# Operand splits on ScalarE and VectorE instead of GpSimd, and two experts of the second chunk in three passes

## The chip, the cores and the metric

The kernel runs on one core of a Trainium2 chip. A core has five engines that work side by side, each through its own queue of instructions in order: TensorE (PE, with PEld for the load of its stationary operand), VectorE (DVE), ScalarE (ACT), GpSimd (POOL) and SyncE (SP, which here only starts DMA transfers). [...] The metric is the device time of one launch in microseconds (us). A lower time is better.

## The reference

Two blocks follow each other.

```python
# attention with sketched features, per batch b (4) and head h (4), 1088 tokens, 32 dimensions
phi(x) = outer(S1 x, S2 x)              # 8 * 8 = 64 features
kv = sum_s phi(k_s) v_s^T ;  z = sum_s phi(k_s)
attn = (phi(q) kv) / (phi(q) z + 1e-6)
x = attn as (4352 tokens, 128)          # heads side by side
# four experts over every token, 128 -> 1024 -> 128
p = domain_probs / (sum of domain_probs + 1e-9)
out = sum_e p[:, e] * (relu(x @ w1[e]) @ w2[e])
```

Everything is float32. Nearly all of the arithmetic is the experts' two products.

## The kernel before, in words

**Tiling.** The 4352 tokens are cut into eleven chunks of 128, 448, 512 (six times), 320, 256 and 128 columns (`CHUNKS`), numbered 0 to 10. For each chunk the kernel walks over 4 experts and, within one, over 4 pairs of 128-wide hidden blocks: `NQ` = 16 steps a chunk, 176 in all, numbered through, so chunk 1 is steps 16 to 31 and chunk 2 begins at step 32. A step i does the first product of two hidden blocks (`first`, j = 0 and 1) and, `LA` = 2 steps behind, the second product of step i-2 (`second`). Between and after the two blocks of a step it writes pieces of the attention (`work`, `piece`): the attention of later tokens runs inside the experts' loop, at a rate worked out from what the coming chunks need. The schedule is written by hand: each engine's queue holds its instructions in the order in which the code writes them.

**Exactness.** In this trace a float32 matmul of 448 columns is followed by the next after 0.750 us, and one of 512 columns on operands of the type fp32r after 0.233 us; the code rounds its operands before it uses that type, hence the splits. Chunks 0 and 10 (`plain`) and chunk 1 (`whole`) use plain float32 matmuls: line 898 for the first product, line 984 for the second. In the others the first product is three fp32r passes over split operands: weights and tokens are each cut into a rounded part and its remainders (`wa`, `wb`, `wd`; `xa`, `xb`, `xd`), line 911 multiplies wa by xa, line 912 wb by xb, ACT scales the sum in place (line 913), and line 931 (`third`) adds wd by xd one block later. Of the second products, those with an even block number (`in_three`) have three passes too (lines 994, 995 and 1001), with hidden values split by ACT (line 935, ha) and DVE (lines 936 and 937, hb and hd in the profile); the odd ones are float32 (line 1001, hid by w_sb).

**Banks.** First products land in four PSUM banks (`ps_h`) that are reused in turn, two a step. In `whole` steps an expert's sum lies in one of two banks, o0 or o1, in turn; with three passes each expert uses both. When an expert closes (`gather`), ACT copies o0 or o1 (line 1028 or 1030), DVE adds o1 (line 1031, three passes only), and POOL multiplies by the gate and adds to the total (lines 1035, 1037, 1038).

**Splitting.** `weight_parts(e)` makes wa, wb and wd of an expert in four steps (two halves); `second_weight_parts(e)` makes vab and vd for the even blocks of w2, writing over buffers of w1 and w2 that are no longer read; `token_parts(m)` makes xa, xb and xd of a chunk. In all three, ACT (line 706, `scaled`, and lines 717, 734, 758) writes scaled copies and rounded parts, and POOL (line 710, `minus`) subtracts. The scaled copies lie in the buffers `ob`, `ev` and `ew`; `ob` and `ev` are those that line 1010 and lines 1028 to 1038 use as well. `to_part` says which expert's splits are written after which step: weights of expert e at steps 16+4e to 19+4e, second weights from step 24+4e. Token splits of chunk m+1 are written after step 12 of chunk m (counted from 0), behind attention pieces that are made up for there.

**Attention on DVE and PE.** Keys: transposes (lines 367, 372), projections on PE (line 410), an addition (420), eight products (425), sums on PE (line 226, in `key_sum`). Queries: a transpose (522), a projection on PE (666), shuffles and an addition (669 to 679), four products qp (535), matmuls n and f (line 226, in `attend`), then division and transposition.

Of the kernel before, what the change touches and what calls it, by code (L numbers as in the profile page):

```python
# [8 lines left out]
F32 = mybir.dt.float32  # L9
BF16 = mybir.dt.bfloat16  # L10
F32R = mybir.dt.float32r
I32 = mybir.dt.int32
ALU = mybir.AluOpType
ACTF = mybir.ActivationFunctionType
# [10 lines left out]
def kernel(  # L25
# [24 lines left out]
    nc = tc.nc  # L50

    P = 128
    HP = 64
    B, H, S, D = q.shape
    E, DM, F = w1.shape
# [6 lines left out]
    NQ = E * FB // 2  # L62
# [636 lines left out]
    wb = cpool.tile([P, E, F], F32R, name="wb")  # L699
    wd = cpool.tile([P, E, F], F32R, name="wd")  # L700

    def scaled(tag, w, scale, dtype=F32):

        t = mpool.tile([P, CW], F32, tag=tag, bufs=1, name="tw")[:, :]
        t = t[:, 0 : w.shape[-1]]
        nc.scalar.activation(t.bitcast(dtype), w, ACTF.Copy, scale=scale)
        return t

    def minus(out, in0, in1):
        nc.gpsimd.tensor_tensor(out=out, in0=in0, in1=in1, op=ALU.subtract)  # L710

    def weight_parts(e):

        HF = F // 2
        for c in (slice(0, HF), slice(HF, F)):
            w, a, b, d = (x[:, c] for x in (w1_of[e], wa[:, e], wb[:, e], wd[:, e]))
            nc.scalar.activation(a, w, ACTF.Copy, scale=4096.0 * NEAR)
            minus(b, scaled("ob", w, 4096.0), a.bitcast(F32))
            yield
            minus(d, b.bitcast(F32), scaled("ev", w, NEAR, F32R))  # L720
            yield


# [3 lines left out]
    def second_weight_parts(e):  # L727

        w = w2_of[e, 0]
        vab = cpool.tile([P, 2, KS * NK * DM], F32R, tag=f"w1_{e}", name="vab")  # L730
        a, b = vab[:, 0], vab[:, 1]
        minus(b, scaled("ob", w, 4096.0), scaled("ev", w, 4096.0 * NEAR, F32R))
        yield
        nc.scalar.activation(a, w, ACTF.Copy, scale=NEAR)
        d = cpool.tile([P, KS * NK * DM], F32R, tag=f"w2_{e}0", name="vd")[:, :]
        minus(d, b.bitcast(F32), a.bitcast(F32))
        w2_parts[e] = a, b, d
        yield

# [13 lines left out]
    def token_parts(m):  # L753

        n = CHUNKS[m]
        xa, xb, xd_ = (mpool.tile([P, CW], F32R, tag=f"x{i}", name=f"x{i}") for i in "abd")
        ((x, _, _),) = placed(START[m], n)
        nc.scalar.activation(xa[:, 0:n], x, ACTF.Copy, scale=R12 * NEAR)
        minus(xb[:, 0:n], x, scaled("ew", x, NEAR, F32R))
        minus(xd_[:, 0:n], xa[:, 0:n].bitcast(F32), xb[:, 0:n].bitcast(F32))  # L760
        xparts[m] = xa, xb, xd_

    def start():

# [76 lines left out]
    def plain(m):  # L841
        return m in (0, NC - 1)

    def whole(m):
        return m == 1

    begun_hp, made_hp = {}, {}

# [12 lines left out]
    def first(i, work, between=None):  # L861

        m, kq = steps[i]
        n, (e, f) = CHUNKS[m], divmod(kq, NP)
        if plain(m):
            third()
            hd = hidden()
            hid[i] = [hd[:, n * j : n * j + n] for j in range(2)]
            if i in begun_hp:
                hp = begun_hp.pop(i)  # L870
                half_columns(i, hp, HP)
            elif i in made_hp:
                hp = made_hp.pop(i)
            else:
                hp = psum(ps_h, "h")
                for j in range(2):
                    both(
                        hp[:, n * j : n * j + n],
                        w1_of[e][:, P * (2 * f + j) : P * (2 * f + j + 1)],
                        (x_last if m else x_first)[:, :],  # L880
                        start=True,
                        stop=True,
                    )
            if m and kq % 2:
                nc.vector.tensor_scalar(
                    out=hd[:, 0 : 2 * n], in0=hp[:, 0 : 2 * n], scalar1=0.0, scalar2=None, op0=ALU.max
                )
            else:
                nc.scalar.activation(hd[:, 0 : 2 * n], hp[:, 0 : 2 * n], ACTF.Relu)
            work()  # L890
            work()
            return
        hid[i] = []
        if whole(m):
            ((x, _, _),) = placed(START[m], n)
            for j in range(2):
                hp = psum(ps_h, "h")[:, 0:n]
                nc.tensor.matmul(hp, w1_of[e][:, P * (2 * f + j) : P * (2 * f + j + 1)], x, start=True, stop=True)
                u = hidden()[:, 0:n]
                nc.scalar.activation(u, hp, ACTF.Relu)  # L900
                hid[i].append(u)
                work()
                if between and j == 0:
                    between(0)
            return
        xa, xb, xd_ = (x[:, 0:n] for x in xparts[m])
        for j in range(2):
            k = 2 * f + j
            g = psum(ps_h, "h")[:, 0:n]
            w = slice(P * k, P * (k + 1))  # L910
            nc.tensor.matmul(g, wa[:, e, w], xa, start=True, stop=False)  # L911
            nc.tensor.matmul(g, wb[:, e, w], xb, start=False, stop=True)  # L912
            nc.scalar.activation(g, g, ACTF.Copy, scale=1.0 + R12)  # L913
            third()
            hid[i].append(None)
            begun.append((i, j, k, g, wd[:, e, w], xd_))
            work()
            if between and j == 0:
                between(0)
# [25 lines left out]
    def second(i, j=None):  # L945
# [4 lines left out]
        if plain(m):  # L950
# [24 lines left out]
                    t, to = (B * S - P, [[DM, P], [1, DM]]) if m else (0, [[G * DM, 32], [1, 4 * DM]])  # L975
                    nc.sync.dma_start(bass.AP(out.tensor, out.offset + t * DM, to), total.pop(m)[:, :])
            return
        if whole(m):
            if f == 0 and j == 0:
                acc[m, e] = None, psum(ps_o, f"o{e % 2}")  # L980
            for j in range(2) if j is None else (j,):
                k = 2 * f + j
                o1 = acc[m, e][1][:, 0:n]
                nc.tensor.matmul(o1, second_weight(e, k), hd[j], start=(k == 0), stop=(k == FB - 1))  # L984
            return
# [82 lines left out]
        begun_hp[i] = psum(ps_h, "h")  # L1068
        half_columns(i, begun_hp[i], 0)
    to_part = {}  # L1070
    for e in range(E):
        for at, parts_of in ((NQ + 4 * e, weight_parts(e)), (NQ + 8 + 4 * e, second_weight_parts(e))):
            for x in range(4):
                to_part.setdefault(at + x, []).append(parts_of)
    ending = iter(())

    def close(i):
# [6 lines left out]
    for i in range(len(steps) + LA):  # L1084
        if i < len(steps):
            m, kq = steps[i]
            while have[0] < START[m] + CHUNKS[m]:
                piece()

            gone = START[m] + CHUNKS[m] * kq / NQ  # L1090
            left = lambda c: START[c] - (4 if c > 1 else 0) * CHUNKS[c - 1] / NQ - gone
            rate = CHUNKS[m] / NQ * max(
                [0] + [(needed[c] + (8 if c > 1 else 4) - done[0]) / left(c) for c in range(m + 1, NC) if left(c) > 0]
            )

            def work():

                if not NQ <= i < NQ + 2:
                    credit[0] = min(credit[0] + rate / 2, 2)
                while credit[0] >= 1:  # L1100
                    credit[0] -= 1
                    piece()

            parted = i >= LA and not plain(steps[i - LA][0]) and not plain(m)
            closing = parted and steps[i - LA][1] % NP == NP - 1

            def between(j):

                if closing:
                    second(i - LA)  # L1110
                    close(i - LA)
                else:
                    second(i - LA, j)

            first(i, work, between if parted else None)
            for parts_of in to_part.get(i, ()):
                next(parts_of, None)
            if kq == NQ - 4 and 0 < m < NC - 2:
                while have[0] < START[m + 1] + CHUNKS[m + 1]:
                    piece()  # L1120
                token_parts(m + 1)
            if i == 2:
                gate_quotients()
            elif i == 5:
                store_gates()
                load_gates(1, range(E))
                load_batch(1)
            if m == NC - 2 and kq == NQ // 2:
                while have[0] < B * S:
                    piece()  # L1130
                load_last()
        if i == LA:

            made_hp[3] = psum(ps_h, "h")
            for c in (0, HP):
                half_columns(3, made_hp[3], c)
        if i >= LA:
            parted = i < len(steps) and parted
            mm, kk = steps[i - LA]
            if parted and closing:  # L1140
                continue
            second(i - LA, 1 if parted else None)
            if kk % NP == NP - 1 and not plain(mm):
                close(i - LA)
            else:
                next(ending, None)
# [29 lines left out]
```

## Time and profile before

| | |
|---|---|
| time, median of 3 runs | 485.01 us (484.96 to 485.11) |
| time of the profiled execution | 485.2 us |
| its span, first to last instruction | 483.4 us |
| TensorE matmuls (PE) busy | 471.4 us, 98% |
| weight loads (PEld) busy | 330.8 us, 68% |
| VectorE (DVE) busy | 327.2 us, 68% |
| ScalarE (ACT) busy | 331.2 us, 69% |
| GpSimd (POOL) busy | 141.9 us, 29% |
| granted TensorE clock | 1.00 |

A line of a group or timeline names the engine, the line of the kernel, the operation and the tiles, written before read. `[0.63 <-ACT h L913]` says that the engine stood idle for 0.63 us until ACT's instruction of line 913 was done. Matmuls are pipelined, so their durations overlap; the distance from start to start tells what one costs. Busy shares are averages over the whole span, and stages differ: between 71 and 84 us, in chunk 1, PE was busy for 13.00 of 13.00 us, POOL for 11.09, ACT for 8.73 and DVE for 0.00; between 96 and 109 us, in chunk 2, PE was busy for 11.09 of 13.00 and DVE for 12.57.

### The profile page before, as it was taken

Reading aid. Unit: us, or ns where it says so; the run is one execution under the profiler, and the core shown is the slowest. Engines: PE = TensorE matmul, PEld = TensorE weight load, DVE = VectorE, ACT = ScalarE, POOL = GpSimd, SP = SyncE. Lnnn points to the kernel's source line nnn. Section 1 sums busy time; section 2 is a strip of 40 time slices with the busy share of each in tenths; the row PEclk is TensorE's granted clock in tenths of the full one; section 3 lists DMA queues with packets and bytes.
Section 4 is the critical chain, followed back from the end, with each engine's and each line's share of the span. In section 5 each row is a group of like instructions: output and inputs, shape, how many; then the busy total and the mean of one; then the engine's idle time right before and its main releaser. Section 6 shows DMA issues by size and latency. Waiting matters only on the chain.

```text
span 483.4 us, 8071 instructions
## 1 busy us (share of the span) xinstructions
PE 471.4 (98%) x2845; PEld 330.8 (68%) x2845; DVE 327.2 (68%) x615; ACT 331.2 (69%) x696; POOL 141.9 (29%) x149
## 2 busy tenths in 40 slices
PE   8999999989999999999999999999999999999997
PEld 5965555656666676666666676667666666888987
DVE  6833250696877769687887669597877686765652
ACT  4366676876857777676857777676877686888841
POOL 5134478432222124211322124212331032232120
PEclk9999999999999999999999999999999999999999
DMA  7827204411101212411103210013102100120710
GB/s 225 273 69 159 66 22 87 97 42 23 44 23 49 45 44 65 118 24 41 41 23 65 45 33 24 22 17 45 38 24 58 29 14 15 34 57 22 244 34 18
DMA packets 45472, 29.19 MB, mean 60 GB/s; under 512 B 26264, under 2 KB 40952, under 8 KB 45432
## 3 DMA queue, kind: packets, MB, share of 16 engines
q1 hardware_dynamic: 45416, 28.68, 23.6%
q8 instruction: 22, 0.36, 0.3%
q14 instruction: 18, 0.15, 0.1%
q10 hardware_dynamic: 16, 0.00, 0.0%
HBM read 24.42 MB, written 4.24 MB: 59 GB/s over the span
## 4 chain that ended last, share of the span: by engine, by line
PE 66%; DVE 6%; ACT 5%; issue 2%; ACTq 0%; DVEq 0%
PE o L1001 23%; PE h L931 10%; PE h L912 8%; PE h L911 8%; PE o L994 5%; PE o L995 5%; ACT h L913 3%; PE n L226 2%; PE h L226 2%; PE o L226 1%; DVE qp L535 1%; DVE hd L937 1%; DVE kp L425 1%; PE f L666 1%; DVE hb L936 1%
## 5 line engine op out<-in xcount | busy, mean ns | idle before, releaser
L913 ACT ACTIVATE h<-h 128x512 f32<-128x512 f32 (+2 forms) x256 | 138.0, 539 | 100.6 <-PE h L912 91.6
L936 DVE SCALAR_TENSOR_TENSOR hb<-h,ha 128x512 fp32r<-128x512 f32 (+2 forms) x128 | 80.8, 631 | 92.3 <-ACT ha L935 91.8
L911 PE MATMUL h<-xa,wa 128*128 128x512 f32 (+2 forms) x256 | 140.5, 549 | 0.0
L1001 PE MATMUL o<-hid,w_sb 128*128 128x512 f32 (+2 forms) x256 | 119.2, 547 | 0.0
L937 DVE SCALAR_TENSOR_TENSOR hd<-ha,hb 128x512 fp32r<-128x512 f32 (+2 forms) x128 | 98.8, 772 | 8.4
L931 PE MATMUL h<-xd,wd 128*128 128x512 f32 (+2 forms) x256 | 98.3, 384 | 3.2 <-ACT h L913 1.5
L912 PE MATMUL h<-xb,wb 128*128 128x512 f32 (+2 forms) x256 | 94.2, 368 | 0.0
L1037 POOL TENSOR_TENSOR ev<-ev,gate 128x512 f32<-128x512 f32 (+3 forms) x27 | 31.3, 1159 | 153.8 <-DVE ev L1031 153.1
L943 ACT ACTIVATE hid<-h 128x512 f32<-128x512 f32 (+2 forms) x128 | 70.2, 548 | 0.2 <-PE h L931 0.2
L935 ACT ACTIVATE ha<-h 128x512 fp32r<-128x512 f32 (+2 forms) x128 | 69.9, 546 | 0.0
L911 PEld LDWEIGHTS h<-xa,wa 128*128 128x128 f32 x256 | 48.2, 188 | 30.1 <-issue 18.6
L912 PEld LDWEIGHTS h<-xb,wb 128*128 128x128 f32 x256 | 48.3, 189 | 29.3 <-issue 23.6
L931 PEld LDWEIGHTS h<-xd,wd 128*128 128x128 f32 x256 | 48.0, 188 | 23.7 <-ACT h L913 16.0
L1001 PEld LDWEIGHTS o<-hid,w_sb 128*128 128x128 f32 x256 | 45.9, 188 | 8.1
L1001 PE MATMUL o<-hd,vd 128*128 128x512 f32 (+2 forms) x128 | 48.3, 378 | 2.7 <-DVE ev L1031 2.7
L994 PE MATMUL o<-ha,vab 128*128 128x512 f32 (+2 forms) x128 | 50.6, 395 | 0.0
L995 PE MATMUL o<-hb,vab 128*128 128x512 f32 (+2 forms) x128 | 47.4, 370 | 0.0
L1038 POOL TENSOR_TENSOR total<-total,ev 128x512 f32<-128x512 f32 (+3 forms) x27 | 35.4, 1313 | 2.1
L535 DVE TENSOR_TENSOR qp<-qa,qb 64x512 f32<-64x512 f32 (+5 forms) x44 | 33.1, 753 | 1.0
L1035 POOL TENSOR_TENSOR total<-ev,gate 128x512 f32<-128x512 f32 (+3 forms) x9 | 10.5, 1163 | 70.3 <-issue 34.0
L1001 PEld LDWEIGHTS o<-hd,vd 128*128 128x128 f32 x128 | 24.0, 187 | 9.3 <-DVE ev L1031 4.5
L984 PE MATMUL o<-hid,w_sb 128*128 128x448 f32 x64 | 28.9, 544 | 0.0
(150 smaller groups left out, 545.4 us busy)
## 6 DMA issues: line engine op xcount, KB each, us to landing
gate<-gates SPq DMA_DIRECT2D x16, 256.0 KB
kn<-in_k_dram SPq DMA_DIRECT2D x4, 544.0 KB
vn<-in_v_dram SPq DMA_DIRECT2D x16, 128.0 KB
w_sb<-in_moe_w_dram SPq DMA_DIRECT2D x4, 512.0 KB
w_sb<-in_moe_w_dram SPq DMA_DIRECT2D x8, 256.0 KB
w_last<-in_moe_w_dram SPq DMA_DIRECT2D x4, 512.0 KB
gate<-gates SPq DMA_DIRECT2D x8, 224.0 KB
qn<-in_q_dram SPq DMA_DIRECT2D x2, 544.0 KB
```

The lines of the kernel that those rows point to most:

```text
L535: nc.vector.tensor_tensor(out=qp[p][64 * x : 64 * x + 64, 0:n], in0=qa[64 * p : 64 * p + 64, 0:n], in1=qb[64 * p : 64 * p + 64, 0:n], op=A ...
L911: nc.tensor.matmul(g, wa[:, e, w], xa, start=True, stop=False)
L912: nc.tensor.matmul(g, wb[:, e, w], xb, start=False, stop=True)
L913: nc.scalar.activation(g, g, ACTF.Copy, scale=1.0 + R12)
L931: nc.tensor.matmul(g, w, x, start=False, stop=True, skip_group_check=True)
L935: nc.scalar.activation(ha, g, ACTF.Relu, scale=NEAR)
L936: nc.vector.scalar_tensor_tensor(out=hb, in0=g, scalar=0.0, in1=high, op0=ALU.max, op1=ALU.subtract)
L937: nc.vector.scalar_tensor_tensor(out=hc, in0=high, scalar=R12, in1=hb.bitcast(F32), op0=ALU.mult, op1=ALU.subtract)
L943: nc.scalar.activation(hid[i][j], g, ACTF.Relu)
L994: nc.tensor.matmul(o0, va[:, w], ha, start=(k == 0), stop=False)
L995: nc.tensor.matmul(o0, vb[:, w], hb, start=False, stop=(k == FB - SK + KS - 1))
L1001: nc.tensor.matmul(o1, w, h, start=(k == 1 and x == 0), stop=(k == FB - 1 and x == len(o1_next) - 1))
```

## The change

GpSimd no longer takes part in the splits, and the scaled copies are gone. `split` is one ACT operation that writes the rounded part; `join` is one DVE operation (scalar_tensor_tensor: scale one input, then add or subtract the other) that writes a remainder. The second remainder (wd, xd) is made from the first two parts, one step later. A weight half thus costs one ACT and two DVE operations, a second weight two and two, a chunk's tokens one and two.

`whole` becomes a property of chunk and expert: in chunk 1 experts 0 and 1 stay in float32, experts 2 and 3 (steps 24 to 31) take the three-pass path. Their parts are needed earlier, so weights are split in the order 2, 3, 0, 1: weights of the x-th in that order at steps 16+4x to 19+4x, second weights from 20+4x. Tokens of chunk 1 are split at steps 20 and 21, those of later chunks at steps 12 and 13 of the chunk before.

```diff
-    def scaled(tag, w, scale, dtype=F32):
-
-        t = mpool.tile([P, CW], F32, tag=tag, bufs=1, name="tw")[:, :]
-        t = t[:, 0 : w.shape[-1]]
-        nc.scalar.activation(t.bitcast(dtype), w, ACTF.Copy, scale=scale)
-        return t
-
-    def minus(out, in0, in1):
-        nc.gpsimd.tensor_tensor(out=out, in0=in0, in1=in1, op=ALU.subtract)
+    def split(a, w, scale):
+        nc.scalar.activation(a, w, ACTF.Copy, scale=scale * NEAR)
+
+    def join(out, in0, scale, in1, op):
+        nc.vector.scalar_tensor_tensor(out=out, in0=in0, scalar=scale, in1=in1, op0=ALU.mult, op1=op)
...
-            nc.scalar.activation(a, w, ACTF.Copy, scale=4096.0 * NEAR)
-            minus(b, scaled("ob", w, 4096.0), a.bitcast(F32))
-            yield
-            minus(d, b.bitcast(F32), scaled("ev", w, NEAR, F32R))
+            split(a, w, 4096.0)
+            join(b, w, -4096.0, a.bitcast(F32), ALU.add)
+            yield
+            join(d, a.bitcast(F32), -R12, b.bitcast(F32), ALU.subtract)
             yield
...
-        minus(b, scaled("ob", w, 4096.0), scaled("ev", w, 4096.0 * NEAR, F32R))
-        yield
-        nc.scalar.activation(a, w, ACTF.Copy, scale=NEAR)
+        split(a, w, 4096.0)
+        join(b, w, 4096.0, a.bitcast(F32), ALU.subtract)
+        yield
+        split(a, w, 1.0)
         d = cpool.tile([P, KS * NK * DM], F32R, tag=f"w2_{e}0", name="vd")[:, :]
-        minus(d, b.bitcast(F32), a.bitcast(F32))
+        join(d, b.bitcast(F32), 1.0, a.bitcast(F32), ALU.subtract)
...
-        nc.scalar.activation(xa[:, 0:n], x, ACTF.Copy, scale=R12 * NEAR)
-        minus(xb[:, 0:n], x, scaled("ew", x, NEAR, F32R))
-        minus(xd_[:, 0:n], xa[:, 0:n].bitcast(F32), xb[:, 0:n].bitcast(F32))
+        split(xa[:, 0:n], x, R12)
+        join(xb[:, 0:n], xa[:, 0:n].bitcast(F32), 4096.0, x, ALU.subtract)
         xparts[m] = xa, xb, xd_
+        yield
+        join(xd_[:, 0:n], xa[:, 0:n].bitcast(F32), 1.0, xb[:, 0:n].bitcast(F32), ALU.add)
+        yield
...
-    def whole(m):
-        return m == 1
+    def whole(m, e):
+        return m == 1 and e < E // 2
...
     to_part = {}
-    for e in range(E):
-        for at, parts_of in ((NQ + 4 * e, weight_parts(e)), (NQ + 8 + 4 * e, second_weight_parts(e))):
-            for x in range(4):
-                to_part.setdefault(at + x, []).append(parts_of)
+    for x, e in enumerate((2, 3, 0, 1)):
+        for at, parts_of in ((NQ + 4 * x, weight_parts(e)), (NQ + 4 + 4 * x, second_weight_parts(e))):
+            for step in range(at, at + 4):
+                to_part.setdefault(step, []).append(parts_of)
+    for m in range(1, NC - 1):
+        at, tokens = NQ * m - 4 if m > 1 else NQ + 4, token_parts(m)
+        for step in (at, at + 1):
+            to_part.setdefault(step, []).append(tokens)
...
             first(i, work, between if parted else None)
-            for parts_of in to_part.get(i, ()):
-                next(parts_of, None)
             if kq == NQ - 4 and 0 < m < NC - 2:
                 while have[0] < START[m + 1] + CHUNKS[m + 1]:
                     piece()
-                token_parts(m + 1)
+            for parts_of in to_part.get(i, ()):
+                next(parts_of, None)
```

More of the change, by code (lines that the diff above doesn't have):

```diff
@@ L893, in first @@
         hid[i] = []
-        if whole(m):
+        if whole(m, e):
             ((x, _, _),) = placed(START[m], n)
@@ L977, in second @@
             return
-        if whole(m):
+        if whole(m, e):
             if f == 0 and j == 0:
```

## The prediction

> **What bounds the kernel now.** I read the page's busy shares first, then TensorE's timeline, because a busy share of 98% can hide anything.
>
> ```profile
> PE 471.4 (98%) x2845; PEld 330.8 (68%) x2845; DVE 327.2 (68%) x615; ACT 331.2 (69%) x696; POOL 141.9 (29%) x149
> ```
>
> TensorE (PE) leads; what counts is how far apart its matmuls start. The timeline of PE, first in the 448-token chunk, then in a 512- and the 320-token chunk (columns: start, duration, engine, line; fp32 matmuls have two records each):
>
> ```profile
> 46.86 0.92 PE L984 MATMUL o<-hid,w_sb 128*128 128x448 f32 x2
> 47.61 0.92 PE L898 MATMUL h<-ring,w_sb 128*128 128x448 f32 x2
> 48.36 0.92 PE L984 MATMUL o<-hid,w_sb 128*128 128x448 f32 x2
> ...
> 204.73 0.40 PE L994 MATMUL o<-ha,vab 128*128 128x512 f32 x1
> 204.96 0.40 PE L995 MATMUL o<-hb,vab 128*128 128x512 f32 x1
> 205.20 0.40 PE L1001 MATMUL o<-hd,vd 128*128 128x512 f32 x1
> ...
> 414.47 0.31 PE L994 MATMUL o<-ha,vab 128*128 128x320 f32 x1
> 414.61 0.31 PE L995 MATMUL o<-hb,vab 128*128 128x320 f32 x1
> ```
>
> Starts, not durations, give the cost: an fp32 matmul of 448 columns takes 0.750 us (46.86 to 47.61 to 48.36); a pass on split operands takes 0.233 us at 512 columns (204.73 to 205.20 in two) and 0.145 at 320. In the 448-token chunk these fp32 matmuls follow each other without a gap.
>
> [...]
>
> Next, the chain that ended last, in order of time, where chunk 2 (512 tokens) has begun, and VectorE (DVE) and GpSimd (POOL) there:
>
> ```profile
> 102.11 0.59 ACT h L913
> 102.70 0.52 ACT ha L935
> 103.22 0.51 ACT vab L734
> 103.73 0.50 ACT h L913
> 104.23 0.68 DVE ev L1031
> 104.91 0.61 DVE hb L936
> ...
> 105.54 1.32 DVE hd L937
> ...
> 106.87 1.68 DVE qp L535
> ...
> 108.60 0.57 PE n L226 x12
> ```
>
> ```profile
> 98.35 0.68 DVE L535 TENSOR_TENSOR qp<-qa,qb 64x512 f32<-64x512 f32 x1
> ...
> 100.45 1.68 DVE L535 TENSOR_TENSOR qp<-qa,qb 64x512 f32<-64x512 f32 x1
> ```
>
> ```profile
> 99.93 1.65 POOL L710 TENSOR_TENSOR vab<-tw 128x512 fp32r<-128x512 f32 x1 [7.14 <-ACT tw L706]
> 105.04 1.27 POOL L1035 TENSOR_TENSOR total<-ev,gate 128x512 f32<-128x512 f32 x1 [3.46 <-PE h L931]
> 106.27 1.72 POOL L710 TENSOR_TENSOR vd<-vab 128x512 fp32r<-128x512 f32 x1
> ```
>
> Here PE is not the bound: the chain runs through ACT and DVE. The same qp multiply costs 0.68 us alone and 1.68 when it starts during a POOL subtract; it ends when POOL's does (100.45+1.68 = 102.1 is 0.5 after 101.58, 106.87+1.67 = 108.5 is 0.5 after 107.99), so DVE sat for about 1 us. Operations that read PSUM (hb, L1031) stay at 0.69.
>
> **The change, part by part.** Step i is one pair of hidden blocks; chunk 1 is steps 16 to 31, chunk 2 starts at step 32.
>
> 1. Passes. Experts 2 and 3 of chunk 1 turn 16 first products and 8 second products from fp32 into three passes. No row has a 448-column pass: the 512 row (0.233) and the 320 row (0.145) bound it, saving 24 x (0.750 - 0.70) = 1.2 to 24 x (0.750 - 0.435) = 7.6 us. Both come to 0.45 ns a column, so I interpolate: 0.204, three are 0.612, saving 24 x 0.138 = **-3.3 us**, all on PE, which is the path there.
>
> 2. Closing an expert. Two experts now use both accumulator banks. In steady chunks each closing delays the third pass: L912 at 200.25, L931 at 200.69, 0.44 for 0.23. Two such: **+0.4** (0 to 1.2, the closing at 101.73 having cost 0.8).
>
> 3. Splits leave POOL. 40 POOL subtracts (0.7 to 1.7 us) and 32 ACT copies (0.63) go; 40 DVE operations come, two SBUF inputs each like L937: 0.69, next start after about 0.62; I use 0.65. What this frees is at 101.7 to 109: PE lost 0.6 at 102.75 (ACT's L1030 had waited 0.76 for POOL's vab, which shared its buffer), 0.35 at 105.05, where it waited for L1031, and 1.05 at 108.60, where two groups of n matmuls that start 0.5 apart elsewhere (49.96, 50.48) start 1.6 apart for want of qp. Of the three long DVE operations there two met POOL subtracts that are gone; the third met L1035, which stays. Steps 36 to 40 get no new DVE work. **-2.0**; bounds -1.0 (without the qp stall) and -2.6 (with the 0.6 that PE lost in the same way at 83 to 89).
>
> 4. Token splits of later chunks, at the 13th and 14th step of each chunk. Before, POOL's two subtracts blocked qp (238.65, 1.68 us) and so L1031, for which PE waited 0.28, 0.48, 0.97 and 0.68 us at four chunk ends, 2.4 together; behind the first of these another qp came 1.0 late for PE (136.08). After, DVE does one 0.65 ahead of L1031 instead of losing 1.0 to 1.4, and the second behind the last qp. I take half of the 2.4 and 0.7 of the 1.0: **-1.9** (0, if the new operation costs as much as the old wait, to -3.4).
>
> 5. The new load on DVE in chunk 1: the waits of before show none, as DVE stood idle for 14.6 us up to 85.55 (the timeline). From the order in which the code writes its pieces, DVE gets in steps 24 to 30, beside the attention's work (L425 at 0.62 to 0.69 each, transposes, adds): hb and hd (0.49 at 320, 0.69 at 512, so 0.6 each, 1.2 a step), and splits, 2, 2, 1, 1, 3, 3 and 1 by step. Sums: step 24, 4.1; 25, 4.0; 26, 2.3; 27, 3.5; 28, 4.4; 29, 5.4 (with L1031); 30, 3.3: 27.0 us. PE needs per step nine passes of 0.204 and one fp32 matmul of 0.750, 2.59, so 18.1 in seven steps, and 2.1 for the attention's L410: 20.2. DVE ends 6.8 us behind, and POOL's L1037 and L1038 of the expert closed at step 29 cost it about 1.5 more, as hd 1.26 and qp 1.67 show at 243.4 to 246.4. The hb of step 30 then lies some 6 to 7 us late, and its h bank (4 of them, two a step) is wanted 1.35 steps after it is written, 3.5 less 1.4 of its own latency: 2.1 us of slack. So PE stalls about **+4.5** at steps 29 to 32. Bounds: 0, if DVE catches up in steps 26 and 31 (1.9 for 3.8) and each operation overlaps the next; and +9, if half of the 13 splits meet POOL and take 1.3 (+4.3). I take 4.5, the plain queue.
>
> The waits that come with it: a split's second half on DVE waits for ACT's first, and behind it wait hb, hd and the attention's products; ACT's second split of a second-layer weight overwrites what DVE's first join reads, so ACT waits for DVE, and behind it L913, for which PE's third pass waits. Both bite only when DVE is late. ACT itself keeps up: its 448-wide operations start 0.43 apart (59.35, 59.78, 60.19), so step 28 has four and three splits of 0.52, 3.3 us for PE's 2.6, once.
>
> Costing nothing: the order 2 3 0 1 (all weights were read in chunk 0, steps 0 to 15, so they are loaded), and DVE's splits in steps 16 to 23 (at most 4.0 us in a 3.0 us step, with 0.65 in steps 22 and 23 and no reader before step 24). No DMA issue moves on SP's queue; POOL's remaining work only gets earlier.
>
> [...]
>
> Sum against the profiled execution's 485.2 us (span 483.4, 1.8 around it): 485.2 - 3.3 + 0.4 - 2.0 - 1.9 + 4.5 = 482.9. It stands 0.2 above the median of 485.01, so **482.7 us**. No change means within 0.2% (484.04 to 485.98), which is about what a measurement can tell.
>
> **Rivals.**
> - DVE's lag is absorbed: the stall is 1, not 4.5: 479.2 us. For it: DVE idles before 64.5 and from 71 to 85. Against: the 27.0 us for 20.2.
> - Slower: DVE's queue becomes the bound of chunk 1, joins meeting POOL at 1.3 us and ACT held behind DVE at the vab overwrite of steps 28 and 29: a stall of 9, 487.2 us. It decides once the stall passes 6.8 (2.9 + 2.0 + 1.9). Against: only one closing falls where the lag is.
> - The passes don't shrink with 448 columns, because a weight load takes 188 ns and hides poorly: 0.233 each, saving 1.2: 484.8 us, no change. Against: at 320 columns passes start 0.145 apart, under 0.188.
>
> **How the numbers follow.** Forecast as summed: 0.52 (own range 481.2 to 484.2, stalls of 3 to 6). Absorbed: 0.20. Slower: 0.18. Passes: 0.10. The range leaves out the best tenth (below 479.0) and the worst (above 486.8). Faster by over 0.2%: 0.45 of the forecast's 0.52, 0.20 and 0.01, so 0.66; slower: 0.04 + 0.15 + 0.01 = 0.20; the rest 0.14.
>
> **What would show it.** Starts of 448-column passes 0.204 apart; L710 gone from POOL and L535 rarely above 0.7 in chunk 2; PE waits at steps 29 to 32 that name DVE hb, ev or kp, some 4.5 us in all; no ACT wait before the first L1030 of chunk 2; L1001's waits on L1031 below 1.3 us in total. I am wrong if PE runs through chunk 1 without waits (faster), or if PE waits on L913 while ACT waits on DVE's vab (slower).

## The result and the profile after

The changed kernel takes 479.56 us (median of four runs, 479.28 to 479.93), the kernel before 485.00 (484.96 to 485.11) beside it: a ratio of 0.9888, 95% interval 0.9871 to 0.9905. The forecast was 482.7. So the sign was right, and the time lies inside the outer bounds (479.0 to 486.8) but below the forecast's own 481.2 to 484.2; the gain, 5.4 us, is more than twice the 2.3 forecast, and the rival "DVE's lag is absorbed" (479.2) comes nearest. The profiled execution took 479.93 us, its span 478.1, at a granted clock of 1.00.

Line numbers are one lower in the changed kernel (L910, L911, L930 are the passes of the first product, L993, L994, L1000 those of the second, L912 ACT's scaling, L1030 DVE's closing add); L703 is `split` on ACT, L706 is `join` on DVE.

The page's busy shares, after:

```profile
PE 467.8 (98%) x2869; PEld 335.1 (70%) x2869; DVE 351.5 (74%) x675; ACT 325.3 (68%) x685; POOL 89.5 (19%) x109
```

POOL lost 52 us of work and DVE took on 24 (42 joins, not 40: chunk 1's tokens have two); PE's busy time fell by 3.6, while the span fell by 5.3. PE's timeline in the 448-token chunk, after:

```profile
67.95 0.36 PE L911 MATMUL h<-xb,wb 128*128 128x448 f32 x1
68.15 0.36 PE L930 MATMUL h<-xd,wd 128*128 128x448 f32 x1
...
68.55 0.37 PE L994 MATMUL o<-hb,vab 128*128 128x448 f32 x1
68.76 0.36 PE L1000 MATMUL o<-hd,vd 128*128 128x448 f32 x1
```

The starts are 0.20 apart, as interpolated, where an fp32 matmul took 0.750. The chain that ended last, after, at the place in chunk 2 where the prediction showed it before:

```profile
102.31 0.69 DVE ev L1030
...
103.64 1.64 DVE hd L936
...
105.29 0.70 DVE qp L535
...
106.04 0.57 PE n L226 x12
```

ACT is gone from it, and qp costs 0.70 where it cost 1.68; hd still meets POOL (1.64). PE's waits in the chunks, first before (5 waits for line 1031, 6 for 913), then after:

```profile
PE o L1001 <- DVE ev L1031: 2.7, 5, 1.0
PE n L226 <- DVE qp L535: 1.7, 2, 0.9
PE h L931 <- ACT h L913: 1.5, 6, 0.6
```

```profile
PE h L930 <- ACT h L912: 1.1, 5, 0.5
PE n L226 <- DVE qp L535: 0.9, 2, 0.6
PE o L1000 <- DVE ev L1030: 0.5, 2, 0.3
PE f L410 <- DVE kT L367: 0.3, 1, 0.3
PE f L410 <- DVE fs L420: 0.2, 1, 0.2
```

The columns are the total, the count and the longest. The waits for the closing add nearly vanish, those for qp halve, and two short ones for the attention's tiles are new, both in chunk 1.

**Where the time went.** The first of each group of query projections (L666) is written once for each later chunk, at the same place in every kernel, so its start on PE is a mark. The table has its start less that of before (us, one profiled execution each; the last row is the difference of the spans):

| mark in before | after | e1 tokens | e2 weights | e3 both splits | e4 passes | e9 |
|---|---|---|---|---|---|---|
| 27.8 | +0.5 | 0.0 | +0.3 | -0.2 | -0.1 | -0.1 |
| 89.6 | -1.0 | +0.8 | -0.5 | -0.9 | +11.1 | -3.1 |
| 118.5 | -2.6 | +0.8 | -1.5 | -2.0 | +9.2 | -4.7 |
| 227.6 | -4.1 | -0.5 | -1.6 | -3.6 | +9.1 | -6.3 |
| 310.3 | -5.9 | -2.3 | -1.8 | -5.3 | +8.9 | -8.0 |
| 375.1 | -5.9 | -2.4 | -1.8 | -5.3 | +8.9 | -8.0 |
| span | -5.3 | -2.2 | -1.7 | -5.1 | +9.0 | -7.7 |

By stage the changed kernel gains 1.5 up to 89.6 (from its own start at 27.8), 1.5 to 118.5, and 3.4 to 375. It loses 0.5 before the first mark, where executions differ (-0.2 to +0.5 in this table) and PE waits 1.5 for a key transpose, and 0.6 after the last.

### The profile page after: what moved, and what is told of

It reads as the page before. It is cut to its first block, busy times and chain, and to the rows that moved or that the text cites. A ratio compares the mean times of both kernels' runs of the same rounds, so it can differ in the third digit from the quotient of the medians.

```text
span 478.1 us, 8123 instructions
## 1 busy us (share of the span) xinstructions
PE 467.8 (98%) x2869; PEld 335.1 (70%) x2869; DVE 351.5 (74%) x675; ACT 325.3 (68%) x685; POOL 89.5 (19%) x109
## 4 chain that ended last, share of the span: by engine, by line
PE 83%; DVE 8%; ACT 5%; issue 2%; DMA 1%; ACTq 0%; SPq 0%; DVEq 0%
PE o L1000 25%; PE h L930 11%; PE h L911 9%; PE h L910 9%; PE o L993 6%; PE o L994 5%; PE h L226 4%; ACT h L912 3%; PE n L226 3%; PE o L226 3%; PE h L897 3%; PE o L983 2%; DVE hd L936 2%; PE f L666 1%; DVE qp L535 1%
## 5 line engine op out<-in xcount | busy, mean ns | idle before, releaser
L912 ACT ACTIVATE h<-h 128x512 f32<-128x512 f32 (+3 forms) x272 | 146.5, 539 | 108.3 <-PE h L911 103.8
L910 PE MATMUL h<-xa,wa 128*128 128x512 f32 (+3 forms) x272 | 149.3, 549 | 0.0
L935 DVE SCALAR_TENSOR_TENSOR hb<-h,ha 128x512 fp32r<-128x512 f32 (+3 forms) x136 | 85.7, 630 | 79.4 <-ACT ha L934 79.1
L1000 PE MATMUL o<-hid,w_sb 128*128 128x512 f32 (+3 forms) x272 | 126.6, 547 | 0.0
L936 DVE SCALAR_TENSOR_TENSOR hd<-ha,hb 128x512 fp32r<-128x512 f32 (+3 forms) x136 | 102.9, 757 | 9.0
L930 PE MATMUL h<-xd,wd 128*128 128x512 f32 (+3 forms) x272 | 104.5, 384 | 2.9 <-ACT h L912 1.1
L911 PE MATMUL h<-xb,wb 128*128 128x512 f32 (+3 forms) x272 | 99.9, 367 | 0.0
L942 ACT ACTIVATE hid<-h 128x512 f32<-128x512 f32 (+3 forms) x136 | 74.6, 549 | 0.2 <-PE h L930 0.2
L934 ACT ACTIVATE ha<-h 128x512 fp32r<-128x512 f32 (+3 forms) x136 | 74.3, 547 | 0.0
L910 PEld LDWEIGHTS h<-xa,wa 128*128 128x128 f32 x272 | 51.2, 188 | 31.4 <-issue 19.6
L911 PEld LDWEIGHTS h<-xb,wb 128*128 128x128 f32 x272 | 51.3, 189 | 31.1 <-issue 25.3
L930 PEld LDWEIGHTS h<-xd,wd 128*128 128x128 f32 x272 | 51.0, 188 | 24.3 <-ACT h L912 16.8
L1000 PEld LDWEIGHTS o<-hid,w_sb 128*128 128x128 f32 x272 | 48.8, 188 | 8.5
L993 PE MATMUL o<-ha,vab 128*128 128x512 f32 (+3 forms) x136 | 53.8, 396 | 0.0
L1000 PE MATMUL o<-hd,vd 128*128 128x512 f32 (+3 forms) x136 | 51.1, 376 | 0.5 <-DVE ev L1030 0.5
L994 PE MATMUL o<-hb,vab 128*128 128x512 f32 (+3 forms) x136 | 50.3, 370 | 0.0
L1037 POOL TENSOR_TENSOR total<-total,ev 128x512 f32<-128x512 f32 (+3 forms) x27 | 36.1, 1337 | 2.1
L1000 PEld LDWEIGHTS o<-hd,vd 128*128 128x128 f32 x136 | 25.5, 188 | 6.1 <-DVE ev L1030 1.6
L993 PEld LDWEIGHTS o<-ha,vab 128*128 128x128 f32 x136 | 25.6, 188 | 4.6 <-issue 1.0
L994 PEld LDWEIGHTS o<-hb,vab 128*128 128x128 f32 x136 | 25.6, 188 | 4.5 <-issue 0.7
```

The source lines that it names most:

```text
L930: nc.tensor.matmul(g, w, x, start=False, stop=True, skip_group_check=True)
L934: nc.scalar.activation(ha, g, ACTF.Relu, scale=NEAR)
L935: nc.vector.scalar_tensor_tensor(out=hb, in0=g, scalar=0.0, in1=high, op0=ALU.max, op1=ALU.subtract)
L936: nc.vector.scalar_tensor_tensor(out=hc, in0=high, scalar=R12, in1=hb.bitcast(F32), op0=ALU.mult, op1=ALU.subtract)
L942: nc.scalar.activation(hid[i][j], g, ACTF.Relu)
L993: nc.tensor.matmul(o0, va[:, w], ha, start=(k == 0), stop=False)
```

## The experiments

The theory after the result: part 5 was mis-sized, since its durations were rows of before, taken while POOL contended; and tokens give more than half of the closing waits. Rivals: the passes gain more than 3.3, or DVE has slack that part 5 did not see.

**e1, tokens alone.** `split` and `join` in `token_parts` of chunks 2 on; weights and chunk 1 as before.

```diff
...
-        minus(xb[:, 0:n], x, scaled("ew", x, NEAR, F32R))
-        minus(xd_[:, 0:n], xa[:, 0:n].bitcast(F32), xb[:, 0:n].bitcast(F32))
+        join(xb[:, 0:n], xa[:, 0:n].bitcast(F32), -4096.0, x, ALU.add)
...
+        yield
+        join(xd_[:, 0:n], xa[:, 0:n].bitcast(F32), 1.0, xb[:, 0:n].bitcast(F32), ALU.subtract)
...
```

> The kernel before with only the token splits of chunks 2 to 9 moved from POOL to ACT and DVE; weights and chunk 1 as before. Ledger theory (the trace after: PE's starts gain 3.4 us between 118 and 375 us, where only the tokens differ): 485.0 - 3.4 = 481.6, and PE's waits for L1031's counterpart below 1 us. Forecast theory (half of the waits go): 485.0 - 1.9 = 483.1.

Measured: 482.96 us (482.66 to 483.15), ratio 0.9955 (0.9941 to 0.9968). From 118.5 on it gains 3.2, as the whole change does (3.4), but it loses 0.8 before 89.6. There DVE meets POOL's weight subtracts, which e1 keeps. DVE's timeline in e1 (L716 is its join):

```profile
74.16 1.35 DVE L716 SCALAR_TENSOR_TENSOR xb<-xa,ring 128x512 fp32r<-128x512 f32 x1 [6.11 <-ACT xa L713]
75.68 2.51 DVE L425 TENSOR_TENSOR kp<-fs 128x320 f32<-128x320 f32 x2
78.11 1.76 DVE L716 SCALAR_TENSOR_TENSOR xd<-xa,xb 128x512 fp32r<-128x512 f32 x1
```

The two products take 1.2 us each here (75.68 to 78.11), and xd 1.76. So the time, near the 483.1 of the theory that half of the waits go, does not speak for it: the wait for the closing add is down to 0.28 (105.83) and 0.17 (241.46), and what is lost lies in chunk 1.

**e2, weights alone.** `split` and `join` in both weight functions; tokens, order and steps as before.

```diff
-            nc.scalar.activation(a, w, ACTF.Copy, scale=4096.0 * NEAR)
-            minus(b, scaled("ob", w, 4096.0), a.bitcast(F32))
+            split(a, w, 4096.0)
+            join(b, w, 4096.0, a.bitcast(F32), ALU.subtract)
...
```

> The kernel before with only the weight splits moved from POOL to ACT and DVE, at the steps and in the order of before; chunk 1 stays float32 and tokens stay on POOL. Ledger theory (PE's starts gain 1.5 between 89 and 118 us): 483.5. Forecast theory: 485.0 - 2.0 = 483.0. A rival, that the new DVE work of steps 24 to 39 costs PE what POOL's absence gives: 485.0, no change.

Measured: 483.83 (483.17 to 484.83), ratio 0.9973 (0.9964 to 0.9981). It gains 0.7 to 89.6 and 1.1 to 118.5, and only 0.3 later. PE's wait for the closing add stays:

```profile
PE o L1008 <- DVE ev L1038: 2.6, 5, 0.8
```

So of the 2.7 us of this wait in before, the 2.4 at the four later chunk ends belong to the token splits alone; the 0.28 at 105.05, in chunk 2, does not (0.28 in e1, 0.39 here). The stage to 118.5 belongs to the weights.

**e3, both splits and no passes.** From the changed kernel: chunk 1 all in float32, weights in the order and at the steps of before, no tokens for chunk 1.

```diff
     def whole(m, e):
-        return m == 1 and e < E // 2
+        return m == 1
...
-    for x, e in enumerate((2, 3, 0, 1)):
-        for at, parts_of in ((NQ + 4 * x, weight_parts(e)), (NQ + 4 + 4 * x, second_weight_parts(e))):
+    for e in range(E):
+        for at, parts_of in ((NQ + 4 * e, weight_parts(e)), (NQ + 8 + 4 * e, second_weight_parts(e))):
...
```

> Weights and tokens split by ACT and DVE at the steps and in the order of before, chunk 1 all float32: the change without its three passes. If the parts add up: ledger theory 485.0 - 3.4 - 1.5 = 480.1, so that the passes bring the remaining 0.5 to 1.5 of the 5.4. Forecast theory, in which the passes bring 2.9 and cost a 4.5 us stall of DVE's queue: this kernel is faster than the changed one, 478.0.

Measured: 480.59 (480.12 to 481.14), ratio 0.9906 (0.9893 to 0.992). The splits alone give 4.6 of the 5.4 us (485.2 less 480.59, against the kernel before of the same chip). So the forecast theory's 478.0, by which the passes cost more than they save, falls. The passes add 1.0 to that, of 3.3 that they take off PE; as the intervals of the two ratios overlap (0.9871 to 0.9905 for the changed kernel), this 1.0 is hardly clear of noise. In chunk 2, where the last two second weights of e3 fall into steps 36 to 39 and the changed kernel has them earlier, e3 gains 1.1 and the changed kernel 1.5.

**e4, passes alone.** The kernel before, with `whole`, order and steps of the change; splits stay on ACT and POOL.

```diff
-    def whole(m):
-        return m == 1
+    def whole(m, e):
+        return m == 1 and e < E // 2
...
+            if i == NQ + 4:
+                token_parts(1)
```

> Experts 2 and 3 of chunk 1 in three passes with weights in the order 2 3 0 1 and tokens of chunk 1 split at step 20, all splits by ACT and POOL as before. Ledger theory: passes bring 3.3 and chunk 1 has no DVE splits, but ACT's scaled copies (0.52 each, more of them) and their waits for POOL lie before L913, so 485.0 - 3.3 + 1 to 4: 483 to 486. If DVE's queue was what cost chunk 1 its stalls in the changed kernel, this one has none there: 482.

Measured: 494.02 (493.43 to 494.19), ratio 1.0181 (1.0167 to 1.0195): 8.8 us slower, far above both theories. PE's waits, then ACT's timeline in e4:

```profile
PE h L931 <- ACT h L913: 10.5, 12, 3.8
```

```profile
82.98 0.63 ACT L706 ACTIVATE tw<-w_sb 128x512 fp32r<-128x512 f32 x1 [3.26 <-POOL total L1038]
83.52 0.53 ACT L913 ACTIVATE h<-h 128x448 f32<-128x448 f32 x1
```

ACT's scaled copy goes into the buffer of the closing sum and waits for POOL; behind it stands the L913 that PE's third pass wants. In part the price goes with the granted clock: it was 0.50 from 79.7 to 89.9, while PE was busy for 6.4 us, and in e5, below, passes that start 0.204 apart at 1.00 start 0.375 apart at 0.50. So with the splits of before the passes do not pay: apart, the passes cost 8.8 and the splits gain 4.6; together they gain 5.4.

**e5 and e6, every join of steps 24 to 30 two and three times.** The repeats write the same values: 13 more operations of 0.60 each, 7.8 us of DVE work, and 15.6.

```diff
     def join(out, in0, scale, in1, op):
-        nc.vector.scalar_tensor_tensor(out=out, in0=in0, scalar=scale, in1=in1, op0=ALU.mult, op1=op)
+        for _ in range(again[0]):
+            nc.vector.scalar_tensor_tensor(out=out, in0=in0, scalar=scale, in1=in1, op0=ALU.mult, op1=op)
...
+            again[0] = 2 if 24 <= i <= 30 else 1
```

> The changed kernel with each of DVE's 13 split operations of steps 24 to 30 written twice (same output, same value): 13 x 0.60 = 7.8 us more DVE work in chunk 1. Plain-queue theory, with the measured lag of 1.7 us at the hb of step 30 and the slack of 2.1 that the forecast gave: all but about 2 us (0.4 slack left and 1.7 that DVE idled at 68 us) lands on PE, 479.5 + 5.8 = 485.3. Rival, that PE has far more slack against DVE than 2.1 us (weights and xd are wanted steps later): at most +2, 481.5.

> The same with each of the 13 written three times, 15.6 us more. Plain queue: the second dose lands in full, 7.8 above the run with two. Rival with more slack: the second dose costs more than the first, and the two costs give the slack (doses 7.8 and 15.6 less what each costs).

Measured: 489.75 (489.26 to 490.31), ratio 1.009 (1.0077 to 1.0103), and 497.76 (497.56 to 498.35), ratio 1.0257 (1.0243 to 1.027). The first 7.8 us cost 10.2 (489.75 less 479.56), the next 8.0. So the rival that more DVE work would be absorbed falls, the second dose lands in full as the plain queue had it, and for the first the plain queue (5.8) comes out too cheap. PE's timeline in e5 shows one reason why the first step costs more than the work added:

```profile
63.26 2.05 PE L410 MATMUL f<-sk,kT 128*128 128x128 f32 x8 [3.51 <-DVE kT L367]
...
65.47 0.57 PE L997 MATMUL o<-hb,vab 128*128 128x448 f32 x1
65.84 0.57 PE L913 MATMUL h<-xa,wa 128*128 128x448 f32 x1
66.22 0.57 PE L914 MATMUL h<-xb,wb 128*128 128x448 f32 x1
```

After a wait of 3.51 us the same passes start 0.375 apart instead of 0.204; the granted clock was 0.50 there (see the last section). The clock's share is large enough to hide some slack of DVE's queue in the first dose; how much slack there was, these two runs do not tell.

**e7, three experts in passes.** Experts 1, 2 and 3; their weights are split from step 12 on.

```diff
-        return m == 1 and e < E // 2
+        return m == 1 and e < 1
...
-    for x, e in enumerate((2, 3, 0, 1)):
-        for at, parts_of in ((NQ + 4 * x, weight_parts(e)), (NQ + 4 + 4 * x, second_weight_parts(e))):
+    for x, e in enumerate((1, 2, 3, 0)):
+        for at, parts_of in ((NQ - 4 + 4 * x, weight_parts(e)), (NQ - 0 + 4 * x, second_weight_parts(e))):
...
-        at, tokens = NQ * m - 4 if m > 1 else NQ + 4, token_parts(m)
+        at, tokens = NQ * m - 4 if m > 1 else 16, token_parts(m)
```

> The changed kernel with experts 1, 2 and 3 of chunk 1 in three passes, weights in the order 1 2 3 0 from step 12 on, tokens of chunk 1 at steps 16 and 17. One more expert saves 12 x 0.138 = 1.65 on PE and costs a closing of 0.2 to 0.4; DVE's and ACT's splits move four steps ahead, into chunk 0, where steps take 0.9 to 1.2 us. If chunk 0 hides them: 479.5 - 1.3 = 478.2, or a little less as chunk 1's burst at step 28 is thinner. If they delay chunk 0's tail: 479 to 481.

Measured: 483.79 (483.56 to 485.93), ratio 0.9976 (0.9963 to 0.9989). Twelve more fp32 matmuls turned into passes would save 1.7 (12 x 0.138); it is 4.2 slower than the changed kernel, and slower than both theories. PE's waits in e7:

```profile
PE f L666 <- DVE qT L522: 2.3, 1, 2.3
PE f L410 <- DVE fs L420: 1.8, 1, 1.8
```

The first ends at 30.16: the joins have moved into chunk 0, where DVE stood idle for 3.92 us before one (wb, 28.80), whose split ACT wrote only at 28.13, after its copies of line 637, and the query transpose (29.40) stood behind it. After it the clock was 0.50 for 3.4 us of work (31.7 to 35.1); by e5's starts, 0.375 apart for 0.204, that is an estimated 1.6 us more, so of the 4.2 a good part is the wait and what the clock adds to it. The price of passes depends on where DVE's work lies.

**e8, tokens of chunk 2 two steps later.** Steps 30 and 31 instead of 28 and 29.

```diff
-        at, tokens = NQ * m - 4 if m > 1 else NQ + 4, token_parts(m)
+        at, tokens = NQ * m - 4 if m > 2 else (NQ + 4, NQ + 14)[m - 1], token_parts(m)
```

> The changed kernel with the tokens of chunk 2 split at steps 30 and 31 instead of 28 and 29. In the trace after, ACT does three splits in a row at 70.49 to 72.05 and PE then waits 0.46 for L912's counterpart of step 29 and loses 0.3 at the next. Theory: one split fewer there saves 0.5, 479.0. Rival: the splits come too close to their use at step 32 and PE waits there instead, 479.5 or more.

Measured: 482.35 (481.43 to 482.97), ratio 0.9935 (0.9923 to 0.9947): 2.8 slower than the changed kernel. PE's waits:

```profile
PE h L911 <- DVE xb L706: 1.9, 1, 1.9
```

Chunk 2's first product (82.66) finds its xb not yet written, as the rival had it; taking work off the crowded steps this way puts it on the path itself. The two executions with the clock at 1.00 took 481.43 and 481.76, about the wait more than the changed kernel; the other three (482.35 to 482.97) had a mean clock of 0.996.

**e9, the splits spread.** Two bursts were named as causes of chunk 1's stalls: the joins of steps 24 and 25, ahead of the first kT and fs, and ACT's three splits at step 28. e9 moves weights into steps 16 to 23, where DVE idles, and the last second weights behind chunk 1.

```diff
+    for make, plan in (
+        (second_weight_parts, {2: (18, 19), 3: (22, 23), 0: (30, 31), 1: (32, 33)}),
+        (weight_parts, {2: (16, 16, 16, 16), 3: (17, 17, 17, 17), 0: (22, 22, 23, 23), 1: (26, 26, 26, 27)}),
+        (token_parts, {1: (20, 21), 2: (28, 29)}),
+    ):
...
```

> The changed kernel with the same splits written at other steps: weights of expert 2 in step 16, of 3 in step 17, second weights of 2 at 18 and 19, second weights of 3 and weights of 0 at 22 and 23, weights of 1 at 26 and 27, second weights of 0 at 30 and 31. DVE gets no split at 24 and 25 and one each at 28 and 29. Queue theory (the passes' gain went into DVE's and ACT's lag in chunk 1): PE's losses there fall from 2.2 us to the 0.5 of the closings, 479.5 - 1.7 = 477.8. Rival (the 2.2 us belongs to the three-pass order of the work itself): 479.5.

Measured: 477.71 (477.46 to 478.11), ratio 0.9837 (0.9822 to 0.9852), the shortest of all, and what the queue theory expected (477.8). PE's waits in the chunks, in e9:

```profile
PE h L930 <- ACT h L912: 1.0, 5, 0.3
PE n L226 <- DVE qp L535: 0.9, 2, 0.6
...
PE o L1000 <- DVE ev L1030: 0.2, 1, 0.2
```

DVE's busy time is the same (351.8 us against 351.5) and PE's two waits in chunk 1, for kT and fs, are gone, and so is the one for ACT at 73.97. To 89.6 e9 gains 3.0 from its own start, the changed kernel 1.5 and e3, without passes, 0.7: of the 3.3 that passes save, 2.3 now arrive instead of 0.8.

**e10 and e11, one burst at a time.** e10 moves only the second weights of expert 0 out of steps 28 and 29; e11 only thins steps 24 and 25.

```diff
 # e10
+        (second_weight_parts, {2: (20, 21), 3: (24, 25), 0: (30, 31), 1: (32, 33)}),
...
 # e11
+        (second_weight_parts, {2: (20, 21), 3: (23, 23), 0: (28, 29), 1: (32, 33)}),
+        (weight_parts, {2: (16, 17, 18, 19), 3: (20, 21, 22, 23), 0: (22, 23, 26, 27), 1: (28, 29, 30, 31)}),
...
```

> The changed kernel with only the second weights of expert 0 moved from steps 28 and 29 to 30 and 31, their use staying at step 34. If the burst of three ACT and three DVE splits at step 28 makes PE wait at steps 29 and 30 (0.46 and 0.3 in the trace after), it saves 0.5: 479.0. If the lag is only passed on to steps 31 and 32: 479.5 or up to 480.5.

> The changed kernel with the second weights of expert 3 moved from steps 24 and 25 to 23, and the first half of expert 0's weights from 24 and 25 to 22 and 23; the rest as it is. If DVE's splits at 24 and 25 are what makes PE wait for kT and fs (0.31 and 0.24, some 0.8 with the restart): 479.5 - 0.8 = 478.7. If not: 479.5.

Measured: 480.02 (479.02 to 480.74), ratio 0.9883 (0.9864 to 0.9902), and 480.21 (479.52 to 481.6), ratio 0.9892 (0.9873 to 0.9912).

**e12, the changed kernel again,** beside e9 to e11.

> The changed kernel itself, on the same chip as the three others, to compare them with: 479.5 by every theory.

Measured: 479.55 (479.34 to 479.9), ratio 0.9875 (0.986 to 0.989). So each half of e9's plan by itself gives nothing in the time that can be told from no change, and both with the rest of the plan give 1.8. In e11 the waits for kT and fs are gone, and PE waits instead for ACT:

```profile
PE h L930 <- ACT h L912: 1.8, 6, 0.7
```

0.67 of this, at 55.78, is new: e11 puts both halves of expert 3's second weights into step 23, ACT's second split waits 0.76 us (54.66) for DVE's join, the overwrite that the prediction had named, and the scaling (55.20) stands behind it. In e10 the waits for kT and fs stay (0.3 and 0.2) and the one for ACT at 73.97 is gone. By the marks, in one execution each, e10 gains 2.1 from 27.8 to 89.6 and e11 1.2, where the changed kernel gains 1.5: e10's move seems to bring within chunk 1 the 0.5 that was expected of it, too little to show in the medians. Which of the plan's further moves (weights of 2 and 3 by steps 16 and 17, those of 1 by 27) carries how much was not separated.

## Why the prediction was off

| term of the sum | predicted | measured |
|---|---|---|
| 1 passes | -3.3 | -3.3 (starts 0.20 apart) |
| 2 and 5, closings and DVE's load | +4.9 | +2.5 |
| 3 splits leave POOL | -2.0 | -0.7 to 89.6, -1.5 to 118.5 |
| 4 tokens | -1.9 | -3.4 |
| start and end of the span | 0 | +1.1 |
| sum | -2.3 | -5.3 |

The +2.5 is what the ledger leaves: 1.5 gained to 89.6, where passes alone would give 3.3 and e2 and e3, which have no passes, gain 0.7 from the weights. The gaps on PE between 53 and 84 add up to 2.2, so the two ways agree within 0.3.

**Part 5 is the step that failed first,** and with part 2 the largest: +4.9 for +2.5. It set 27.0 us of DVE work against 20.2 on PE. The queue was the right picture, its durations were not: they were rows of before in which POOL's subtracts, which the change removes, held DVE up. DVE's and POOL's timelines, before:

```profile
65.54 2.50 DVE L425 TENSOR_TENSOR kp<-fs 128x256 f32<-128x256 f32 x4
68.21 2.77 DVE L425 TENSOR_TENSOR kp<-fs 128x320 f32<-128x320 f32 x4
```

```profile
66.29 1.46 POOL L710 TENSOR_TENSOR wb<-tw,wa 128x512 fp32r<-128x512 f32 x1 [0.73 <-ACT tw L706]
...
69.06 1.57 POOL L710 TENSOR_TENSOR wd<-wb,tw 128x512 fp32r<-128x512 f32 x1 [1.31 <-ACT tw L706]
```

(of these eight products the median took 0.49 us and the longest, beside a subtract, 1.56), and after, in the steps that had been summed:

```profile
72.19 0.42 DVE L425 TENSOR_TENSOR kp<-fs 128x256 f32<-128x256 f32 x1
72.52 0.68 DVE L706 SCALAR_TENSOR_TENSOR vab<-w_sb,vab 128x512 fp32r<-128x512 f32 x1
73.12 0.69 DVE L706 SCALAR_TENSOR_TENSOR wb<-w_sb,wa 128x512 fp32r<-128x512 f32 x1
...
74.58 0.49 DVE L425 TENSOR_TENSOR kp<-fs 128x320 f32<-128x320 f32 x1
74.99 0.61 DVE L1030 TENSOR_TENSOR ev<-ev,o 128x448 f32<-128x448 f32 x1
...
76.17 1.13 DVE L936 SCALAR_TENSOR_TENSOR hd<-ha,hb 128x448 fp32r<-128x448 f32 x1
77.23 1.44 DVE L425 TENSOR_TENSOR kp<-fs 128x320 f32<-128x320 f32 x1
```

L425 had been charged at 0.62 to 0.69; from start to next start it takes 0.33 at 256 columns and 0.41 at 320, eight of them 3.0 us instead of 5.3. A join takes 0.60 (72.52 to 73.12), not 0.65. The 1.5 us lost to POOL's closing operations was right: hd 0.5 and L425 0.95 too long (76.17, 77.23). That makes 27.0 - 2.3 - 0.65 + 1.5 = 25.5 us, against 20.5 on PE; less the 2.1 of slack, 2.9 by the prediction's own rule. That this is near the 2.2 to 2.5 measured is luck, for the slack and the place were wrong too: no wait at steps 29 to 32 names hb, ev or kp. Step 30's ha and hb, and the first product of step 32 and PE's use of that hb:

```profile
76.11 0.57 ACT L934 ACTIVATE ha<-h 128x448 fp32r<-128x448 f32 x1
...
81.20 0.61 DVE L935 SCALAR_TENSOR_TENSOR hb<-h,ha 128x448 fp32r<-128x448 f32 x1
```

```profile
80.35 0.74 PE L910 MATMUL h<-xa,wa 128*128 128x512 f32 x1
...
82.97 0.36 PE L994 MATMUL o<-hb,vab 128*128 128x448 f32 x1
```

The hb came 4.5 us after its ha was done (76.68 to 81.20; they are the seventh of each in chunk 1, and the 1.7 in what was expected of e5 paired it with the eighth ha). That is more than twice the slack, yet PE did not stall: step 32 began its first product at 80.35, before this hb had read its bank, so it took another one. The banks are thus not reused strictly in turn, as the slack assumed, and PE asked for the hb only at 82.97. The waits came earlier and by another road, for kT and fs at 60.6 and 65.4, and for ACT, which had three splits ahead of the scaling that PE's third pass needs:

```profile
70.49 0.63 ACT L703 ACTIVATE vab<-w_sb 128x512 fp32r<-128x512 f32 x1
...
71.53 0.63 ACT L703 ACTIVATE xa<-ring 128x512 fp32r<-128x512 f32 x1
...
73.36 0.56 ACT L912 ACTIVATE h<-h 128x448 f32<-128x448 f32 x1
```

```profile
73.16 0.36 PE L911 MATMUL h<-xb,wb 128*128 128x448 f32 x1
73.97 0.47 PE L930 MATMUL h<-xd,wd 128*128 128x448 f32 x1 [0.46 <-ACT h L912]
```

The prediction had seen step 28 ask 3.3 us of ACT for PE's 2.6 and charged nothing for it, as it comes once; ACT, busy from 69.63 on without a gap, passed it on to PE, which started L930 0.6 late there and the next one, at 75.38, 0.3 late. An expert closes at the same place (ACT's copy L1029 at 72.94), so part of the 0.6 is the closing of part 2. ACT does not wait on DVE's vab, as the slower rival had it.

**Part 4 was too cautious.** It took half of the 2.4 us of closing waits and 0.7 behind qp. Nearly all of the 2.4 went (e1, e3 and the changed kernel gain 3.2 to 3.4 from 118.5 on; e2, with POOL's token subtracts, 0.3): a join of 0.6 ahead of the closing add makes it late at one chunk end alone, by 0.17, since DVE no longer stands blocked for 1.0 to 1.4 behind it. Behind qp the gain was smaller than the 0.7: that wait fell from 0.82 (136.08) to 0.58 (132.71).

**Part 3 was about right:** 2.2 in all for 2.0, with the 0.6 near 83 to 89 that had been set as its far bound. Its reading of qp holds: the stall of 1.05 fell to 0.5, and what stays is the long hd at 103.64, under POOL's closing product, as had been said of L1035. The closing before it costs PE 0.2 beyond a pass (starts at 100.68 and 101.12) where it had cost 0.8.

**The two rivals.** "Lag is absorbed" has the nearest time, and in part its reason holds: the late hb of step 30 stalled nothing. But 2.5 us of stall remain at other places, not 1, and e5 and e6 show that more DVE work is not absorbed; that it comes so near, because part 4 gave 1.5 more, is luck. "Slower" named the bound on DVE's queue that e5 and e6 bring about (in e4 it is ACT that waits, for POOL), and "passes don't shrink" is refuted by the starts.

## What to carry to other kernels

In these traces a duration held for the company that the operation had: after, L425 at 320 columns took 0.49 us by itself (74.58) and 1.44 beside POOL's L1037 (77.23). When the change removes an engine that contended, price the remaining work by the shortest rows of the same shape and add the contention that stays as a separate term. When an engine is near full, write down its work step by step, and look at every burst at once when work is moved to where it idles: e9's plan gave 1.8 us, while e11, which thinned one burst, made a new wait for ACT. And a change of two parts needs each part run alone; here one alone costs 8.8 us and the other gains 4.6, and the sum says nothing of the pair.

## What the runs showed of the hardware

In the profiled executions of e4 to e7 the granted clock of TensorE fell to 0.50 after stretches in which PE had been busy for 0.24 to 1.80 of 3.40 us. Windows of e5, then of e7 (columns: stretch, its length, busy time and count of PE, PEld, DVE, ACT and POOL, granted clock, DMA share, GB/s):

```profile
58.20:61.60 3.40, 1.45 (x6) 0.75 (x4) 3.33 (x4) 2.84 (x6) 2.66 (x2) 1.00 0.36 77
61.60:68.40 6.80, 5.14 (x20) 4.96 (x21) 6.45 (x11) 1.35 (x3) 0.34 (x1) 0.50 0.25 77
```

```profile
28.30:31.70 3.40, 1.54 (x10) 0.71 (x10) 2.87 (x6) 1.80 (x5) 0.00 (x0) 0.99 0.05 8
31.70:35.10 3.40, 3.40 (x8) 1.18 (x4) 0.57 (x1) 0.54 (x1) 0.00 (x0) 0.50 0.43 134
```

In e5 the clock fell at 61.6, during the wait of 3.51 us that ended at 63.26, and was 0.50 until 68.4, though PE worked from 63.26 on. Waits of up to 1 us, in the kernels before and after, left it at 1.00 in these chunks, and so did one of 1.91 in e8's profiled execution (three of e8's other executions, with a mean of 0.996, suggest that it did not always). In e5 it fell again from 82.1 to 88.9, after waits of 0.45 and 0.73 us and at the beginning of one of 2.22; in e4 at 79.7, after waits of 2.21 and 0.45 and before the longest; in e7 at 31.7, when PE had stood idle once, for 2.29 us, and was at work again. In the 3.4 us before these four drops (as long as e7's slow stretch, 31.7 to 35.1) PE was busy for 1.45, 1.75, 1.78 and 1.54 us, and before the two of e6 (at 63.0 and 83.4) for 0.24 and 1.80. In the trace after it was busy for 1.95 of the 3.4 us from 2.9 to 6.3, with a wait of 1.45, and the clock stayed at 1.00. What decides between the two was not shown. In e5 the passes after the first stall started 0.375 us apart for 0.204, so it cost more than its own length. PE was busy there for 5.14 us of the first slow stretch and for 5.31 of the second; if all of its work stretched as those passes did, the two hold some 4.8 us less of it, twice the surplus of e5 (10.2 us for 7.8 of DVE work). That is an estimate from these numbers, and no run separates it from the waits.
